# The order of softplus and a softmax split on ACT, and the queue of the state's first 128 rows

## The chip, the core and the metric

The kernel runs on one core of a Trainium2 chip. The metric is the time of one execution in microseconds, as the device measures it; the median of three runs stands for a kernel. The core's engines are TensorE (PE; its weight loads are shown as PEld), VectorE (DVE), ScalarE (ACT), GpSimd (POOL) and SyncE (SP). Each works through its own instructions in order and waits for the others by semaphores. DMA transfers are issued here from the queues of SP, ACT and POOL.

## What is computed

The reference has three stages on 8 images of 512 tokens with 512 features (8 heads of 64), and 32 state rows for each image:

```python
scores = scale * x @ state.T;  a = softmax(scores);   xread = a @ state     # per head
scores2 = scale * state @ x.T; a2 = softmax(scores2); sread = a2 @ x
x = concat([xread, sread])                     # 8 * (512 + 32) = 4352 rows of 512
h = x @ w_in;  g = max(h, 0) + log1p(exp(-abs(h)));  y = g @ w_out          # softplus MLP
logits = y @ w_gate     # each row goes to one of 8 experts, at most 544 rows each, greedily by logit
out = relu(y[rows] @ w1[e]) @ w2[e]            # per expert
```

Results are float32. The kernel gets that accuracy out of TensorE by splitting operands in two parts, `hi` and `lo`, and making three products: hi·hi, hi·lo and lo·hi.

## The kernel before, in words

**The middle stage.** The MLP runs in slots. Slot s is batch b = s // 16 (one image) and ft = s % 16 (128 of the 2048 hidden features). For a slot, `mlp1` makes the hidden values of 128 features and 512 tokens in a PSUM bank `p_h` with six matmuls (line 485). They aren't made from w_in but from the token softmax (`at_hi`, `at_lo`) and a product of state and w_in (`P_hi`, `P_lo`). There are two banks p_h, so that slots s and s + 2 share one. Softplus follows in three ACT operations and one on DVE: `softplus_abs` writes abs(h) to `t_sp` (line 520) and puts it on the list `waits`; `softplus_log` empties the list and makes Exp and Ln of each entry (lines 527 and 528); `softplus_b` makes g = max(h, 0) + t_sp on DVE (line 540), which is the last reader of the bank. ACT then copies g to `g_hi` (line 548), POOL makes `g_lo` = g − g_hi (line 551), and `mlp2` adds twelve matmuls into four banks p_y (lines 569, 571, 573).

**The order of the work** is that of the program: the loop over s (line 793) is written out by hand, and each engine executes what it is given in that order. For batches after the first, the body of slot s is, in short:

```python
softplus_b(s + 1); mlp1(s + 2); softplus_abs(s + 2)
if ft % 4 == 0: p_pair()                    # P_hi on ACT, P_lo on DVE (lines 454 to 462)
if ft in (ATT if b > 1 else ATT1): att_step(b)
softplus_log()                              # Exp and Ln of slot s + 2
mlp2(s)
```

`att_step` advances the attention of the next image by one step. For images 2 to 7 that is the generator `attention`, run during batches 1 to 6. Its steps are: scores; two steps that subtract the maximum and make Exp (these call `softplus_log` ahead of their own Exp); two steps that divide by the sum on DVE (lines 287 to 290), transpose into `back` on DVE (line 291), copy to `at_hi` on ACT (line 292) and make `at_lo` on POOL (line 293): these two are the splits of the token softmax, for the even and the odd heads; a step for the state softmax (maximum on DVE at lines 295 and 296, `softplus_log`, Exp on ACT at line 299, sums on DVE); transposes of it on TensorE (line 308); and the read of x by the state. In batches 2 to 6 the splits fall in slots ft = 7 and 8; in batch 1 they fall later, in slots 9 and 10. `at_hi` and `at_lo` of an image are read by `mlp1` of the next batch.

**The state rows.** The 256 rows of all states go through the MLP as a batch of their own, 128 rows (j = 0, 1) at a time. In the generator `mlp2_rest` (line 757) their pieces, each one block of 128 features for one j, run through `split_g` (ACT's g_hi, POOL's g_lo) and three matmuls (lines 576, 578, 580); the split of a piece is issued one piece ahead, and g_hi and g_lo have two buffers. Behind the last piece of each j, `y_state(j)` copies the bank to `yt` on DVE (line 631) and sends it to `y_d` in DRAM in four transfers of 64 KB, one for each image (line 634). These pieces are mixed by hand with the routing of the first expert (lines 912 to 1088), whose steps alternate between DVE and small matmuls. When the first expert is known, SP reads its number and loads its w1 (line 1106); when its rows are known, POOL gathers them from `y_d` (line 1122), which needs all rows of y to have landed. The expert stage follows.

Of the kernel before, what the change touches and what calls it, by code (L numbers as in the profile page):

```python
# [17 lines left out]
B, H, S, NS, D = 8, 8, 512, 32, 64  # L18
# [12 lines left out]
def attn_moe_kernel(ctx, tc, x_s, x_t, state_t, w_in, w_out, w_gate, w1, w2, out):  # L31
    nc = tc.nc
    V, A, G, PE, SP = nc.vector, nc.scalar, nc.gpsimd, nc.tensor, nc.sync
# [12 lines left out]
    def bg(kind=None):  # L46

        if turn_of[1]:
            turn_of[0] ^= 1
            kind = turn_of[0]  # L50
        return bank("bg1" if kind else "bg0")
# [76 lines left out]
    y_d = dram.tile([N, DM], F32, name="y_d")  # L128
# [86 lines left out]
    def ordered(x):  # L215

        return x.rearrange("p (j q c) -> p q j c", j=4, q=4)
# [34 lines left out]
    def attention(b):  # L252

        xT = XT.pop(b)
        ST = at.tile([128, 2, 512], F32, name="ST", tag="ST")
        Z = at.tile([128, 2, 512], F32, name="Z", tag="P1")
        m2 = at.tile([128, 2], F32, name="m2", bufs=2)
        s2 = at.tile([128, 2], F32, name="s2", bufs=2)
        hi = pt.tile([128, 2, 512], F32R, name="at_hi", bufs=2)
        lo = pt.tile([128, 2, 512], F32R, name="at_lo", bufs=2)  # L260
        AT[b] = (hi, lo)
        ps = bg(0), bg(1)
        for par in range(2):
            o = par * 64
            for hp in range(4):
                PE.matmul(ps[par][hp * 32:(hp + 1) * 32, :], stT[o:o + 64, b, hp, :], xT[o:o + 64, hp, :],
                          start=True, stop=True, tile_position=(o, hp * 32))
        for par in range(2):
            A.activation(ST[:, par], ps[par], AF.Copy)
        xt = at.tile([128, 4, DM], F32, name="xt", tag="x")  # L270
        SP.dma_start(xt, x_s[b].rearrange("(r p) c -> p r c", p=128))
        yield
        G3 = [128, 16, NS]
        for par in range(2):
            a3 = Z[:, par].rearrange("p (g n) -> p g n", n=NS)
            m1 = at.tile([128, 16], F32, name="m1", bufs=2)
            V.transpose(Z[:, par], ST[:, par])
            V.tensor_reduce(m1, a3, axis=AX, op=OP.max)
            V.tensor_tensor(a3, a3, m1[:, :, None].to_broadcast(G3), op=OP.subtract)
            softplus_log()  # L280
            A.activation(Z[:, par], Z[:, par], AF.Exp, scale=0.125)
            yield
        back = wk.tile([128, 2, 512], F32, name="back", tag="yst", bufs=4)
        for par in range(2):
            a3 = Z[:, par].rearrange("p (g n) -> p g n", n=NS)
            s1 = at.tile([128, 16], F32, name="s1", bufs=2)
            V.tensor_reduce(s1, a3, axis=AX, op=OP.add)
            V.tensor_scalar(s1, s1, 1e-9, None, op0=OP.add)
            V.reciprocal(s1, s1)
            V.tensor_tensor(a3, a3, s1[:, :, None].to_broadcast(G3), op=OP.mult)  # L290
            V.transpose(back[:, par], Z[:, par])
            A.activation(hi[:, par], back[:, par], AF.Copy)
            G.tensor_tensor(lo[:, par], back[:, par], hi[:, par].bitcast(F32), op=OP.subtract)
            yield
        V.tensor_reduce(m2, ST, axis=AX, op=OP.max)
        V.tensor_scalar(m2, m2, -0.125, None, op0=OP.mult)
        softplus_log()
        for par in range(2):
            A.activation(ST[:, par], ST[:, par], AF.Exp, bias=m2[:, par:par + 1], scale=0.125,
                         accum_out=s2[:, par:par + 1])  # L300
        V.tensor_scalar(s2, s2, 1e-9, None, op0=OP.add)
        V.reciprocal(s2, s2)
        yield
        A2 = at.tile([128, 2, 512], F32, name="A2", tag="P1")
        ps = bg(0), bg(1)
        for par in range(2):
            for r in range(4):
                PE.transpose(ps[par][:, r * 128:(r + 1) * 128], ST[:, par, r * 128:(r + 1) * 128], ident)
        for par in range(2):
            A.activation(A2[:, par], ps[par], AF.Copy)  # L310
        yield
        yield from state_read(b, A2, xt, s2)

    def state_read(b, A2, xt, s2):
        p = bg()
        for par in range(2):
            for r in range(4):
                for hp in range(4):
                    c0 = r * 128 + hp * 32
                    PE.matmul(p[hp * 32:(hp + 1) * 32, par * 64:(par + 1) * 64], A2[:, par, c0:c0 + 32],  # L320
                              xt[:, r, (2 * hp + par) * D:(2 * hp + par + 1) * D], start=(r == 0), stop=(r == 3))
        if b + 1 < B:
            load_xT(b + 1)
        sr = at.tile([128, 128], F32, name="sr")
        for par in range(2):
            V.tensor_scalar(sr[:, par * 64:(par + 1) * 64], p[:, par * 64:(par + 1) * 64], s2[:, par:par + 1],
                            None, op0=OP.mult)
        yield
        p = bg()
        PE.transpose(p[:, 0:128], sr, ident)  # L330
        V.tensor_copy(XsT[:, :, b * NS:(b + 1) * NS], p[:, 0:128].rearrange("p (h n) -> p h n", h=4))
# [192 lines left out]
    def softplus_log():  # L524
        while waits:
            t = waits.pop(0)
            A.activation(t, t, AF.Exp, scale=-1.0)  # L527
            A.activation(t, t, AF.Ln, bias=1.0)  # L528
# [100 lines left out]
    def y_state(j):  # L629
        t = wk.tile([128, 2, 512], F32, name="yt", tag="yst", bufs=4)  # L630
        V.tensor_copy(t[:, 0].rearrange("p (q j c) -> p q j c", q=4, j=4), ordered(yb[j]))
        for i in range(4):
            r0 = (4 * j + i) * TB + S
            (SP if i % 2 else A).dma_start(y_d[r0:r0 + NS], t[i * NS:(i + 1) * NS, 0])

    def logits(s, kind=None):
        b, ft = divmod(s, NFT)
# [119 lines left out]
    def mlp2_rest():  # L757
        todo = [(s, (0, 1, 2, 3)) for s in range(NX - LATE, NX)]
        todo += [(NX + ft, (j,)) for j in range(2) for ft in range(NFT)]

        def split(i):
            if i < len(todo):
                s, js = todo[i]
                split_g(s, late[s] if s < NX else stash["g"][:, s - NX], slice(js[0] * 128, js[-1] * 128 + 128),
                        LATE_ON[i] if i < LATE else "AG")

        split(0)
        yield
        for i, (s, js) in enumerate(todo):
            split(i + 1)  # L770
            while s == NX and len(lazy) > 3 - js[0]:
                lazy.pop(0)()
            if s == NX - 1:
                adds = y_out(B - 1, 0) + y_out(B - 1, 2)
            for j in js:
                for i_, _ in enumerate(mlp2_steps(s, (j,))):
                    if i_ == 2 and s == NX - 1:
                        lazy.append(adds[j])
                    yield
            if s == NSLOT - 1:  # L780
                y_state(js[0])
# [590 lines left out]
```

## Time and profile before

| | |
|---|---|
| median of 3 runs | 1225.92 us (1225.27 to 1227.36) |
| profiled execution | 1226.8 us, span 1225.0 us |
| busy share of the span | PE 95%, PEld 74%, DVE 54%, ACT 52%, POOL 40% |
| mean granted TensorE clock | 0.99 |
| instructions | 21305 |

The span runs from the first to the last instruction of the core; the execution's time has some 1.8 us more around it. An engine's busy time is the union of its instructions; matmuls are pipelined and their ends are modelled, so two that follow one another overlap in the rows. A timeline row is: start, duration, engine, line, operation, out<-in, shape, count, and in brackets the idle time of the engine before it with what ended it. A "q" behind an engine's name means its queue, which issues a transfer. A row of the costliest groups is: line, engine, operation, names, shape, count | busy us, mean ns of one | idle us before it, with what ended most of it. A granted clock of 1.00 is 2.4 GHz, one of 0.5 is 1.2 GHz.

### The profile page before, as it was taken

The numbers are of one execution on the slowest core, as the hardware profiler recorded it, in microseconds if no ns is written. First come the engines' busy times: TensorE is split into PE (matmuls) and PEld (weight loads), VectorE is DVE, ScalarE is ACT, GpSimd is POOL, SyncE is SP. The second block draws the span as 40 slices with busy tenths as digits, with TensorE's granted clock in tenths as the row PEclk, the third lists the DMA queues.
The fourth block names the chain that finished last, engine by engine and source line by source line (L and its number), as shares of the span: only waits on it lengthen the run. The fifth ranks groups of instructions, "written<-read, shape, count | busy, mean of one in ns | idle before, by whom it ended". The sixth has DMA issues, their size and how long they took to land.

```text
span 1225.0 us, 21305 instructions
## 1 busy us (share of the span) xinstructions
PE 1159.3 (95%) x8291; PEld 910.3 (74%) x8291; DVE 667.3 (54%) x1797; ACT 639.2 (52%) x1277; POOL 487.8 (40%) x466
## 2 busy tenths in 40 slices
PE   4898999999999999999999997999999999999996
PEld 1565676777677776777677765879797988789895
DVE  6998545353363543634434266777685868751120
ACT  3776656666666666666666732533343333333330
POOL 0334323222232232222344425645647555546531
PEclk9998999999999999999999998999999999999999
DMA  7463021111201112002000003251523415234200
GB/s 241 139 202 127 1 70 35 53 52 36 69 1 52 52 35 58 13 36 69 1 18 18 1 18 123 88 194 40 180 92 129 150 68 172 104 108 140 89 18 37
DMA packets 51061, 95.78 MB, mean 78 GB/s; under 512 B 4624, under 2 KB 19088, under 8 KB 50960
## 3 DMA queue, kind: packets, MB, share of 16 engines
q1 hardware_dynamic: 45136, 76.33, 18.8%
q0 software_dynamic: 5632, 17.83, 4.2%
q8 instruction: 65, 1.06, 0.4%
q10 hardware_dynamic: 192, 0.26, 0.1%
q14 instruction: 36, 0.29, 0.1%
HBM read 76.58 MB, written 17.83 MB: 77 GB/s over the span
## 4 chain that ended last, share of the span: by engine, by line
PE 66%; DVE 17%; ACT 7%; issue 6%; POOL 2%; DMA 1%; SPq 0%; ACTq 0%; POOLq 0%; DVEq 0%
PE p_y L1310 12%; PE p_h L485 10%; PE p_y L1265 6%; PE p_y L569 6%; PE p_y L571 5%; PE p_h L1265 5%; PE p_y L573 5%; PE p_bg L912 2%; DVE g L540 2%; PE p_y L576 2%; PE p_bg L454 2%; PE p_bg L496 2%; PE p_y L578 2%; PE p_y L580 2%; PE p_h L1176 1%
## 5 line engine op out<-in xcount | busy, mean ns | idle before, releaser
L551 POOL TENSOR_TENSOR g_lo<-g,g_hi 128x512 fp32r<-128x512 f32 x127 | 164.9, 1299 | 340.7 <-ACT g_hi L548 327.3
L569 PE MATMUL p_y<-g_hi,wo_hi 128*128 128x512 f32 x448 | 185.0, 413 | 0.0
L571 PE MATMUL p_y<-g_hi,wo_lo 128*128 128x512 f32 x448 | 177.7, 397 | 3.7 <-POOL wo_lo L232 3.7
L573 PE MATMUL p_y<-g_lo,wo_hi 128*128 128x512 f32 x448 | 177.2, 396 | 0.0
L540 DVE SCALAR_TENSOR_TENSOR g<-p_h,t_sp 128x512 f32<-128x512 f32 x128 | 87.7, 686 | 122.7 <-ACT t_sp L528 121.8
L548 ACT ACTIVATE g_hi<-g 128x512 fp32r<-128x512 f32 x126 | 79.6, 632 | 124.0 <-DVE g L540 95.2
L569 PEld LDWEIGHTS p_y<-g_hi,wo_hi 128*128 128x128 f32 x448 | 85.1, 190 | 48.3 <-issue 15.9
L485 PE MATMUL p_h<-at_hi,P_hi 128*128 128x512 f32 x256 | 104.9, 410 | 8.1 <-DVE g L540 8.1
L1310 PE MATMUL p_y<-w2h,h2h 128*128 128x512 f32 x256 | 105.1, 411 | 0.0
L485 PE MATMUL p_h<-at_hi,P_lo 128*128 128x512 f32 x256 | 101.8, 398 | 0.0
L485 PE MATMUL p_h<-at_lo,P_hi 128*128 128x512 f32 x256 | 101.7, 397 | 0.0
L1310 PE MATMUL p_y<-w2l,h2h 128*128 128x512 f32 x256 | 101.5, 396 | 0.0
L1310 PE MATMUL p_y<-w2h,h2l 128*128 128x512 f32 x256 | 101.3, 396 | 0.0
L571 PEld LDWEIGHTS p_y<-g_hi,wo_lo 128*128 128x128 f32 x448 | 85.4, 191 | 21.0 <-POOL wo_lo L232 4.9
L573 PEld LDWEIGHTS p_y<-g_lo,wo_hi 128*128 128x128 f32 x448 | 85.2, 190 | 21.0 <-POOL g_lo L551 2.4
L1318 POOL DMA_INDIRECT out_dram<-ot,idx x40 | 39.4, 985 | 145.6 <-ACT ot L1316 68.9
L1149 POOL TENSOR_TENSOR w2l<-s2w,w2h 128x512 fp32r<-128x512 f32 x64 | 82.5, 1305 | 14.2 <-ACT w2h L1148 13.0
L520 ACT ACTIVATE t_sp<-p_h 128x512 f32<-128x512 f32 x128 | 75.3, 588 | 24.5 <-PE p_h L485 24.2
L1149 POOL TENSOR_TENSOR w1l<-s1w,w1h 128x512 fp32r<-128x512 f32 x63 | 80.4, 1300 | 11.2 <-ACT w1h L1148 10.3
L528 ACT ACTIVATE t_sp<-t_sp 128x512 f32<-128x512 f32 x128 | 80.9, 632 | 4.1
L527 ACT ACTIVATE t_sp<-t_sp 128x512 f32<-128x512 f32 x128 | 80.6, 630 | 2.0
L1265 PE MATMUL p_y<-yTh,w1h 128*128 128x288 f32 (+1 forms) x256 | 76.9, 300 | 0.6 <-DVE h2t L1274 0.6
(284 smaller groups left out, 2643.5 us busy)
## 6 DMA issues: line engine op xcount, KB each, us to landing
s1w<-in_moe_w_dram SPq DMA_DIRECT2D x8, 2048.0 KB, 8.4
s2w<-in_moe_w_dram SPq DMA_DIRECT2D x8, 2048.0 KB, 9.5
st<-in_moe_w_in_dram SPq DMA_DIRECT2D x16, 512.0 KB, 4.1
xT<-in_x_t_dram SPq DMA_DIRECT2D x16, 512.0 KB, 4.4
st<-in_moe_w_out_dram SPq DMA_DIRECT2D x16, 512.0 KB, 3.7
xt<-in_x_s_dram SPq DMA_DIRECT2D x8, 1024.0 KB, 5.8
y_d<-yz SPq DMA_DIRECT2D x48, 128.0 KB, 3.6
y_d<-s_g SPq DMA_DIRECT2D x8, 128.0 KB, 2.2
```

Source lines behind the costliest of these rows:

```text
L485: PE.matmul(h, l[:, f0:f0 + 128], r[:, par, :], start=(n == 0), stop=(n == 5))
L527: A.activation(t, t, AF.Exp, scale=-1.0)
L528: A.activation(t, t, AF.Ln, bias=1.0)
L540: V.scalar_tensor_tensor(g[:, :w], hps.pop(s)[:, :w], 0.0, tsp.pop(s)[:, :w], op0=OP.max, op1=OP.add)
L548: A.activation(hi[:, c], g[:, c], AF.Copy)
L551: (G if on[1] == "G" else V).tensor_tensor(lo[:, c], g[:, c], hi[:, c].bitcast(F32), op=OP.subtract)
L569: PE.matmul(yb[j], wo_hi[:, ft, c], hi, start=st, stop=False)
L571: PE.matmul(yb[j], wo_lo[:, ft, c], hi, start=False, stop=False)
L573: PE.matmul(yb[j], wo_hi[:, ft, c], lo, start=False, stop=sp)
L1149: eng.tensor_tensor(lo, src, hi.bitcast(F32), op=OP.subtract)
L1265: PE.matmul(p[:, :w], l[:, k, f], r[:, k, c], start=(n == 0), stop=(n == 11))
L1310: PE.matmul(p, l[:, ft, c], r[:, ft, :], start=(n == 0), stop=(n == 23))
```

## The change

In the two split steps of `attention`, `softplus_log()` is called ahead of ACT's copy to `at_hi`, so that the pending Exp and Ln of slot s + 2 stand ahead of that copy in ACT's order; the call behind `att_step` then finds an empty list. In `y_state`, all four transfers for j = 0 are issued by SP (before: images 1 and 3 of the four by SP, 0 and 2 by ACT); for j = 1, SP issues 0 and 2 and ACT issues 1 and 3 (before: the other way round).

```diff
             V.transpose(back[:, par], Z[:, par])
+            softplus_log()
             A.activation(hi[:, par], back[:, par], AF.Copy)
             G.tensor_tensor(lo[:, par], back[:, par], hi[:, par].bitcast(F32), op=OP.subtract)
             yield
...
         V.tensor_copy(t[:, 0].rearrange("p (q j c) -> p q j c", q=4, j=4), ordered(yb[j]))
         for i in range(4):
             r0 = (4 * j + i) * TB + S
-            (SP if i % 2 else A).dma_start(y_d[r0:r0 + NS], t[i * NS:(i + 1) * NS, 0])
+            (A if j and i % 2 else SP).dma_start(y_d[r0:r0 + NS], t[i * NS:(i + 1) * NS, 0])
```

## Rows read from the trace of the kernel before

**Rows 1.** The page's first part: busy us, share of the span, instructions.
```profile
PE 1159.3 (95%) x8291; PEld 910.3 (74%) x8291; DVE 667.3 (54%) x1797; ACT 639.2 (52%) x1277; POOL 487.8 (40%) x466
```
**Rows 2.** Busy time by stretch: one batch, and the start of the expert stage.
```profile
core 0: us, PE busy (x) PEld busy (x) DVE busy (x) ACT busy (x) POOL busy (x), PEclk, DMA share, GB/s
...
503.00:581.00 78.00, 76.87 (x453) 56.40 (x452) 34.74 (x63) 50.66 (x95) 23.05 (x18) 1.00 0.12 41
...
757.00:775.00 18.00, 9.84 (x75) 8.54 (x72) 13.36 (x39) 5.68 (x11) 11.96 (x11) 0.72 0.63 191
```
**Rows 3.** The costliest groups: the first matmul of p_h.
```profile
L485 PE MATMUL p_h<-at_hi,P_hi 128*128 128x512 f32 x256 | 104.9, 410 | 8.1 <-DVE g L540 8.1
```
**Rows 4.** Line 292, what ended ACT's idle time before it (us, times).
```profile
  DVE back L291: 26.8, 12
```
**Rows 5.** Timeline of batch 6, second split: ACT, VectorE, POOL, then TensorE.
```profile
585.81 0.58 ACT L520 ACTIVATE t_sp<-p_h 128x512 f32<-128x512 f32 x1
...
590.92 0.63 ACT L292 ACTIVATE at_hi<-back 128x512 fp32r<-128x512 f32 x1 [3.05 <-DVE back L291]
...
592.84 0.69 DVE L540 SCALAR_TENSOR_TENSOR g<-p_h,t_sp 128x512 f32<-128x512 f32 x1 [1.95 <-ACT t_sp L528]
...
597.82 0.67 DVE L540 SCALAR_TENSOR_TENSOR g<-p_h,t_sp 128x512 f32<-128x512 f32 x1
...
591.63 1.28 POOL L293 TENSOR_TENSOR at_lo<-back,at_hi 128x512 fp32r<-128x512 f32 x1 [4.36 <-ACT at_hi L292]
...
592.35 0.39 PE L573 MATMUL p_y<-g_lo,wo_hi 128*128 128x512 f32 x1
593.59 0.50 PE L485 MATMUL p_h<-at_hi,P_hi 128*128 128x512 f32 x1 [0.85 <-DVE g L540]
...
595.09 0.39 PE L569 MATMUL p_y<-g_hi,wo_hi 128*128 128x512 f32 x1
595.32 0.39 PE L571 MATMUL p_y<-g_hi,wo_lo 128*128 128x512 f32 x1
595.72 0.50 PE L573 MATMUL p_y<-g_lo,wo_hi 128*128 128x512 f32 x1
...
597.91 0.40 PE L573 MATMUL p_y<-g_lo,wo_hi 128*128 128x512 f32 x1
598.55 0.50 PE L485 MATMUL p_h<-at_hi,P_hi 128*128 128x512 f32 x1 [0.25 <-DVE g L540]
```
**Rows 6.** Timeline of batch 6, first split: ACT's copy and VectorE's next g.
```profile
582.54 0.63 ACT L292 ACTIVATE at_hi<-back 128x512 fp32r<-128x512 f32 x1 [1.43 <-DVE back L291]
...
584.46 0.69 DVE L540 SCALAR_TENSOR_TENSOR g<-p_h,t_sp 128x512 f32<-128x512 f32 x1 [1.96 <-ACT t_sp L528]
```
**Rows 7.** Timeline of batch 1: TensorE's two pauses behind its splits.
```profile
210.31 0.50 PE L485 MATMUL p_h<-at_hi,P_hi 128*128 128x512 f32 x1 [1.11 <-DVE g L540]
...
218.20 1.06 PE L308 MATMUL p_bg<-ident,ST 128*128 128x128 f32 x8 [0.87 <-DVE P_lo L462]
```
**Rows 8.** Timeline around `y_state(0)`: VectorE, ACT with its queue, SP's queue, TensorE.
```profile
743.13 0.69 DVE L631 COPY yt<-p_y 128x512 f32<-128x512 f32 x1
743.85 0.84 ACTq L634 DMA_DIRECT2D y_d<-yt  x2
744.79 0.51 ACT L548 ACTIVATE g_hi<-s_g 128x128 fp32r<-128x128 f32 x2 [3.06 <-DVE yt L631]
...
750.14 0.41 SPq L1106 DMA_DIRECT2D s1w<-in_moe_w_dram  x1
...
743.40 0.40 PE L580 MATMUL p_y<-wo_hi,g_lo 128*128 128x512 f32 x1
745.16 0.49 PE L576 MATMUL p_y<-wo_hi,g_hi 128*128 128x512 f32 x1 [1.36 <-ACT g_hi L548]
```
**Rows 9.** Timeline at `y_state(1)`: the two queues' issues.
```profile
757.24 1.19 SPq L634 DMA_DIRECT2D y_d<-yt  x2
757.25 1.39 ACTq L634 DMA_DIRECT2D y_d<-yt  x2
```

## The prediction

> **What bounds the kernel now.** The page comes first: TensorE is busy 95% of the span [rows 1]. An average hides stages, so the table of stretches comes next [rows 2]. In one batch of the middle stage (503 to 581 us) TensorE is busy 76.87 of 78 us at a granted clock of 1.00, ACT 50.66, VectorE 34.74, POOL 23.05. No other engine is near its limit, so there is nothing to win but TensorE's own pauses and nothing to lose unless another engine makes it wait. Which pauses? The costliest groups name one: the first matmul of p_h (line 485) was idle for 8.1 us, all of it until VectorE had written g [rows 3]. I then looked for who makes g late. The split of the token softmax (line 292) holds ACT idle for 26.8 us in 12 places, waiting for the transpose `back` [rows 4]. Twelve is two splits in each of six batches (b = 1 to 6, which prepare images 2 to 7).
>
> The timeline of one such batch joins the two [rows 5]. ACT finishes Abs of slot 10 by about 586.4, then copies P, and is idle from 587.87 (590.92 less 3.05). The split's copy stands next in its queue and can't start until 590.92. Exp and Ln of slot 10 stand behind it, though their input was ready more than 4 us before. VectorE has finished `back` just ahead of 590.92 and idles 1.95 us until Ln ends; it writes g at 592.84 to 593.53. TensorE needs that, because p_h has two banks and the matmuls of slot 12 take the bank that g of slot 10 reads. It starts at 593.59.
>
> **What TensorE loses there.** Matmuls of this kind start 0.23 us apart (595.09 to 595.32), so a pause is the distance of two starts less 0.23; the first matmul after a pause also lasts 0.50 instead of 0.40, which I count as 0.10 more. All in [rows 5]:
> - 592.35 to 593.59: 1.24 − 0.23 = 1.01, and 0.10: 1.11 (waits for g of slot 10).
> - 595.32 to 595.72: 0.17, and 0.10: 0.27 (waits for g_lo of slot 10, made late by the same g).
> - 597.91 to 598.55: 0.41, and 0.10: 0.51 (waits for g of slot 11, which ends at 598.49).
> Sum 1.89 us. I take the other batches but the first as alike: 0.85 and 0.25 us of idle, five times, make 5.5 of the 8.1 in [rows 3]. Batch 1 does its attention steps later and adds 1.11 [rows 7]; what is left, some 1.4, lies ahead of these batches.
>
> **The change, part one: Exp and Ln ahead of the split.** It adds and removes no operation. In 12 places two ACT operations of 0.63 us move ahead of one copy, and the flush at the end of the slot then finds nothing to do.
>
> First split of a batch [rows 6]: the copy starts at 582.54 after 1.43 us of idle, and Exp and Ln need 1.28, so they fit into the idle and the copy loses nothing. g of slot 9, at 584.46 after 1.96 us of waiting, comes at about 582.5. TensorE doesn't wait for that one today, so I count 0; it is slack for the next slot.
>
> Second split: Exp and Ln fit into 3.05 us of idle, g of slot 10 follows `back` at about 590.9 and ends at 591.6. TensorE wants the bank at 592.35 + 0.23 = 592.58: a full us to spare. The 1.11 goes.
>
> What is late next? On ACT g_hi of slot 10 follows the split's copy and ends near 592.3. POOL makes at_lo from 591.63 for 1.28 us, and g_lo of slot 10 queues behind it: at the 1.28 of its neighbour, 592.95 to 594.25. TensorE wants it at 595.55 − 1.11 = 594.44. This is the tightest place, 0.2 us; of the 1.96 us by which the first split's g comes earlier some should reach it, but I don't count on that. I take the 0.27 as gone. g of slot 11 moves with g of slot 10 by 1.95, to 596.54; TensorE wants it at 598.14 − 1.38 = 596.76. I take the 0.51 as gone too. The bounds for these two are 0 and 0.78 per batch. Nothing else is queued behind the split's copy that anybody needs soon: at_hi and at_lo are read one batch later.
>
> Five batches: 5 × 1.89 = 9.45. Batch 1 [rows 7]: 1.11 of idle before the matmul at 210.31, with the 0.16 by which the modelled end of a matmul (0.39) runs beyond its 0.23 and 0.10 for the first matmul, is 1.37; the transposes at 218.20 wait for P_lo 0.87 + 0.16 = 1.03, P_lo being late because the same chain made ACT's P copies late. Here g moves by nearly 2 us at both splits, so I count both: 2.40. Part one: 11.85 us, with 1.11 × 5 + 1.37 = 6.92 as the lower bound if only the first pause goes.
>
> **Part two: the state's rows.** For the first 128 rows two of four transfers move from ACT's queue to SP's; for the second 128 each queue keeps two, exchanged. The row that matters is ACT's next split of g: it starts at 744.79 after 3.06 us of idle that ended with the copy to yt at 743.13 to 743.82, and two issues of 0.84 us together [rows 8]. TensorE's next piece waits for it: 743.40 to 745.16 is 1.76, less 0.23 is 1.53, and 0.10 for the first matmul: 1.63. Without the issues ACT waits neither for yt nor for them, and its split follows the matmul that frees g_hi, as in the pieces before. The routing chain, whose matmul of `sat` stands behind it on TensorE, comes earlier by the same. Taken: 1.63.
>
> The price is on SP: four issues at some 0.4 us end near 745.5. Behind them stands the load of the first expert's w1 at 750.14 [rows 8], some 748.5 when all has moved. So they hide in 3 us of an idle queue; without that cover they would cost 0.8. The second 128 rows: SP's pair takes 1.19 us and ACT's 1.39 [rows 9], so the exchange moves the last landing, for which the gather waits, by 0.2 either way; I take 0.
>
> The Trainium skill's page "DMA: Bandwidth & Descriptors", section "Issuing engines are not separate DMA queues", says that a second issuing engine saves only the sequencer's time of issuing. By that rule the move is worth ACT's 0.84 us at most and costs SP as much; the rows differ, because ACT's issues also wait for yt with g_hi behind them.
>
> **Sum:** 11.85 + 1.63 = 13.48, taken as 13.5. The profiled execution took 1226.8 us, 0.9 above the median of the runs, 1225.92. So 1213.3 for a profiled execution and **1212.4** for the median.
>
> **The rivals.**
> - *Only the first pause goes.* POOL's queue or the chain of g of slot 11 stays as late as now: 6.92 + 1.63 = 8.55, 1217.4 us. For it: only 0.2 us to spare at two points. Against: what the first split gives comes on top.
> - *Part two saves issue time alone.* ACT's split would be late for another reason: 11.85 + 0.84 = 12.7, 1213.2. Against: the split of every other piece comes in time without it.
> - *Part one does nothing.* If the list of pending operations were empty at the split, only part two is left: 1224.3. Against: Abs stands ahead of the copy and g waits for Ln behind it [rows 5].
> - *Slower, by the clock.* The granted clock falls to 0.72 on average at 757 to 775 [rows 2], which is half speed (1.2 of 2.4 GHz) for 10 of 18 us; TensorE is busy for 9.84 of them. Everything is moved by 13.5 us, so the clock could come back later than the matmuls. Matmuls at half speed lose half their time: from 27 us of dense matmuls at 1.2 GHz on, the gain is lost; with 40 us it is 1225.9 − 13.5 + 20 = 1232.4. Against: 8 us of this stretch are at full speed already, and nothing in the change lengthens the wait in it.
>
> **How the numbers follow.** Forecast 0.67, issue time alone 0.08, first pause alone 0.16, nothing from part one 0.05, slower 0.04. The forecast's own spread is some 2 us, mostly the stretch at half clock: 1210 to 1214.5. The range reaches to the first rival, 1210 to 1218. What a measurement can tell from no change is about 0.2%, 2.5 us: the first three cases are faster by more, 0.91; the fourth is the same by it, 0.05; the last slower, 0.04.
>
> **What would show it.** Right: in the changed profile ACT's copy of line 292 follows Ln; its idle time falls from 26.8 to some 11 us; the 8.1 us of [rows 3] fall to about 1.4; a batch is 1.9 us shorter; in the batch's waits neither g_lo nor P_lo takes TensorE's time; the matmul of the second state half follows without 1.36 us of idle; SP issues four transfers in a row. Wrong: a new TensorE wait for g_lo at the third matmul of a slot, a P copy or g still late after the split, w1 of the first expert landing later against the routing, or a stretch at half clock behind 775 us.

## The result and the profile after

| | before | changed |
|---|---|---|
| median of 5 runs each, side by side | 1227.09 us (1225.27 to 1227.69) | 1214.73 us (1214.45 to 1214.99) |
| profiled execution, span | 1225.0 us | 1212.9 us |
| mean granted TensorE clock | 0.99 | 0.988 |

The ratio is 0.9902 with a 95% interval of 0.9888 to 0.9915: faster by 12.4 us in the medians and by 12.1 in the two spans. The forecast was 13.5 faster, 1212.4 us.

The page of the changed kernel, its first part and the group that answers to [rows 3] (all its line numbers from 292 on are one higher):

```profile
PE 1156.4 (95%) x8291; PEld 913.0 (75%) x8291; DVE 663.3 (55%) x1797; ACT 641.0 (53%) x1277; POOL 488.6 (40%) x466
...
L486 PE MATMUL p_h<-at_hi,P_hi 128*128 128x512 f32 x256 | 103.9, 406 | 1.4 <-DVE g L541 1.4
```

The idle time ahead of the first matmul of p_h has gone from 8.1 to 1.4 us. The table of stretches for [rows 2], with the columns as there: first a stretch of one batch's length, taken 7 us earlier, then the start of the expert stage:

```profile
496.00:574.00 78.00, 78.00 (x462) 58.21 (x461) 35.23 (x64) 52.52 (x98) 23.80 (x19) 1.00 0.13 41
...
744.00:763.00 19.00, 10.81 (x66) 9.64 (x67) 13.21 (x38) 5.70 (x11) 12.98 (x11) 0.64 0.61 183
```

In 78 us TensorE is now busy for all 78.00 (76.87 before) and makes 462 matmuls instead of 453. The second row is no better than before: the mean granted clock is 0.64 over 19 us where it was 0.72 over 18.

What ended ACT's idle time before the split's copy, for [rows 4]:

```profile
  DVE back L291: 11.7, 7
```

The timeline of batch 6 in the changed kernel, second split, for [rows 5] (ACT and VectorE, then POOL, then TensorE):

```profile
577.97 0.63 ACT L529 ACTIVATE t_sp<-t_sp 128x512 f32<-128x512 f32 x1
579.73 0.71 DVE L291 STREAM_TRANSPOSE back<-Z 128x512 f32<-128x512 f32 x1
580.36 0.65 DVE L541 SCALAR_TENSOR_TENSOR g<-p_h,t_sp 128x512 f32<-128x512 f32 x1
580.47 0.63 ACT L293 ACTIVATE at_hi<-back 128x512 fp32r<-128x512 f32 x1 [1.87 <-DVE back L291]
...
581.18 1.30 POOL L294 TENSOR_TENSOR at_lo<-back,at_hi 128x512 fp32r<-128x512 f32 x1 [5.25 <-ACT at_hi L293]
582.44 1.30 POOL L552 TENSOR_TENSOR g_lo<-g,g_hi 128x512 fp32r<-128x512 f32 x1
...
582.49 0.39 PE L574 MATMUL p_y<-g_lo,wo_hi 128*128 128x512 f32 x1
582.72 0.40 PE L486 MATMUL p_h<-at_hi,P_hi 128*128 128x512 f32 x1
584.35 0.40 PE L572 MATMUL p_y<-g_hi,wo_lo 128*128 128x512 f32 x1
584.58 0.39 PE L574 MATMUL p_y<-g_lo,wo_hi 128*128 128x512 f32 x1
```

Ln ends at 578.60, VectorE writes g straight behind `back`, and the copy comes last. The two pauses of TensorE are gone: 582.49 to 582.72 and 584.35 to 584.58 are both the plain 0.23.

The state's last piece of the first 128 rows, for [rows 8] (VectorE, ACT, SP's queue, TensorE):

```profile
731.20 0.31 ACT L549 ACTIVATE g_hi<-s_g 128x128 fp32r<-128x128 f32 x1 [1.23 <-PE p_y L579]
731.37 0.69 DVE L632 COPY yt<-p_y 128x512 f32<-128x512 f32 x1
732.09 1.75 SPq L635 DMA_DIRECT2D y_d<-yt  x4
736.70 0.41 SPq L1107 DMA_DIRECT2D s1w<-in_moe_w_dram  x1
...
731.64 0.39 PE L581 MATMUL p_y<-wo_hi,g_lo 128*128 128x512 f32 x1
731.86 0.39 PE L577 MATMUL p_y<-wo_hi,g_hi 128*128 128x512 f32 x1
```

ACT splits g before the copy to yt has even begun, the matmul follows after 0.22, and SP's four issues end at 733.84, 2.86 us ahead of the next thing in its queue.

**The two traces laid side by side.** The matmuls are the same 8291 in the same order, so each can be compared with its own counterpart. The table sums up by how much a matmul starts earlier (−) or later (+) in the changed trace:

| where (start before → after) | step | stands at |
|---|---|---|
| up to batch 1 | +0.16 | +0.16 |
| batch 1: 210.31 → 209.29, 218.20 → 216.05 | −1.18, −1.13 | −2.15 |
| batches 2 to 6, five times −1.10, −0.25, −0.56 | −9.54 | −11.69 (598.55 → 586.86) |
| second half of the state: 745.16 → 731.86 | −1.60 | −13.29 |
| first gathered rows: 764.68 → 752.49 | +1.11 | −12.19 |
| matmuls at half clock, up to 771.38 → 760.18 | +0.99 | −11.20 |
| matmul of `sat`: 773.90 → 761.80 | −0.90 | −12.10, and so to the end |

Each row gives the shift at the matmul named. Since the first matmul behind a pause lasts longer, the shift settles some 0.1 us further in the next few matmuls: it is −2.20 behind batch 1, −11.74 ahead of the state's second half and −13.39 ahead of the first gathered rows.

The gain was all there and 1.2 us of it was lost again at the start of the expert stage. The timeline there, changed kernel: the last copy to yt with ACT's issues behind it, two VectorE operations of the routing (`oh`, and `mk`, which compares scores `v` with thresholds `thr`), POOL's `w1l` (the lo part of the expert's first weights) and the first gather:

```profile
743.12 0.69 DVE L632 COPY yt<-p_y 128x512 f32<-128x512 f32 x1
743.85 1.41 ACTq L635 DMA_DIRECT2D y_d<-yt  x2
...
746.03 0.44 DVE L985 TENSOR_TENSOR oh<-oh,code 128x272 f32<-128x272 f32 x1
746.07 1.52 POOL L1150 TENSOR_TENSOR w1l<-s1w,w1h 128x512 fp32r<-128x512 f32 x1 [3.53 <-ACT w1h L1149]
...
747.81 1.24 DVE L1016 TENSOR_TENSOR mk<-v,thr 128x1054 bf16<-128x1054 f32 x1
747.88 2.18 POOL L1123 DMA_INDIRECT xg<-y_d,idx  x1 [0.29 <-DVE ohu L990]
```

and the kernel before:

```profile
756.52 0.69 DVE L631 COPY yt<-p_y 128x512 f32<-128x512 f32 x1
...
761.15 1.14 POOL L1122 DMA_INDIRECT xg<-y_d,idx  x1 [0.18 <-issue]
761.20 1.24 DVE L1015 TENSOR_TENSOR mk<-v,thr 128x1054 bf16<-128x1054 f32 x1
```

Before, POOL's first gather starts 0.05 us ahead of VectorE's mk and takes 1.14; after, it starts 0.07 behind it and takes 2.18. The 0.12 us of order cost 1.04, and the five gathers run one after another, so the later ones, and the transposes of their rows on TensorE, are late by about the same.

### The profile page after: what moved, and what is told of

It reads as the page before. It is cut to its first block, busy times and chain, and to the rows that moved or that the text cites. A ratio compares the mean times of both kernels' runs of the same rounds, so it can differ in the third digit from the quotient of the medians.

```text
span 1212.9 us, 21304 instructions
## 1 busy us (share of the span) xinstructions
PE 1156.4 (95%) x8291; PEld 913.0 (75%) x8291; DVE 663.3 (55%) x1797; ACT 641.0 (53%) x1277; POOL 488.6 (40%) x466
## 4 chain that ended last, share of the span: by engine, by line
PE 77%; DVE 12%; issue 6%; POOL 2%; ACT 1%; DMA 1%; SPq 0%; POOLq 0%; DVEq 0%; ACTq 0%
PE p_h L486 13%; PE p_y L1311 12%; PE p_y L570 8%; PE p_y L572 8%; PE p_y L574 8%; PE p_y L1266 6%; PE p_h L1266 5%; PE p_bg L455 2%; PE p_bg L913 2%; PE p_y L577 2%; PE p_bg L497 2%; PE p_y L579 2%; PE p_y L581 2%; PE p_h L1177 1%; DVE c_a L193 1%
## 5 line engine op out<-in xcount | busy, mean ns | idle before, releaser
L1150 POOL TENSOR_TENSOR w1l<-s1w,w1h 128x512 fp32r<-128x512 f32 x63 | 80.4, 1300 | 11.3 <-ACT w1h L1149 10.4
```

The lines of the kernel that those rows point to most:

```text
L1150: eng.tensor_tensor(lo, src, hi.bitcast(F32), op=OP.subtract)
```

## The experiments

Two questions were open: whether each part gives what the forecast gave it, and what made the first gather late. A useful measure for the second, free of everything ahead of it, is the time from the last copy to yt until the end of the span: 1225.0 − 756.52 = 468.5 us before, 1212.9 − 743.12 = 469.8 after. In the traces of the last two sessions this stretch also holds pauses near 960 us, whether a gather was held or not ("What stays open"). Free of these too is the distance from that copy to the matmul of `sat` (a step of the routing), where the table ends: 773.90 − 756.52 = 17.38 before, 761.80 − 743.12 = 18.68 after. The runs were made in three sessions, each on one chip with its own runs of the kernel before; a ratio compares within a session.

### One part at a time

First the order of the softplus alone, the line of `y_state` as before:

```diff
-            (A if j and i % 2 else SP).dma_start(y_d[r0:r0 + NS], t[i * NS:(i + 1) * NS, 0])
+            (SP if i % 2 else A).dma_start(y_d[r0:r0 + NS], t[i * NS:(i + 1) * NS, 0])
```

> Part one alone (the queues of the state rows as before). The forecast's theory: TensorE's pauses in batches 1 to 6 are gone, the pause of 1.36 us at the second state half is back; 11.7 us less than before, by what the traces of before and after show up to 600 us: ratio 0.9905. If the two parts help each other (part one's gain needs part two), less than 11 us. Theory of the late gather (the first gather on POOL starts just behind VectorE's mk and is held by it, because the second state half's rows land later): with the old queues the first gather takes 1.1 to 1.2 us, not 2.2.

Measured: 1215.18 us against 1227.3, ratio 0.9901 (0.9886 to 0.9916): 12.1 us faster. TensorE's timeline at the second half of the state:

```profile
732.40 0.39 PE L581 MATMUL p_y<-wo_hi,g_lo 128*128 128x512 f32 x1
734.15 0.50 PE L577 MATMUL p_y<-wo_hi,g_hi 128*128 128x512 f32 x1 [1.37 <-ACT g_hi L549]
```

The pause of [rows 8] is back, to 0.01 us (1.75 from start to start). The first gather took 1.14 us here, and from the copy to yt to the end it is 1214.1 − 745.49 = 468.6, as before (17.43 to `sat`).

Then the queues alone, in the kernel before:

```diff
-            (SP if i % 2 else A).dma_start(y_d[r0:r0 + NS], t[i * NS:(i + 1) * NS, 0])
+            (A if j and i % 2 else SP).dma_start(y_d[r0:r0 + NS], t[i * NS:(i + 1) * NS, 0])
```

> Part two alone. If its two effects are the 1.6 us pause that goes and a first gather of 2.2 us in place of 1.1: 0.5 us less than before, which can hardly be told from no change. If the long gather has nothing to do with the queues: 1.6 us less, and a first gather of 1.1 us. If the move saves issue time alone: 0.8 us less, with TensorE's pause halved and not gone.

Measured: 1225.83 us, ratio 0.9991 (0.9982 to 1.0): 1.5 faster in the medians, which the interval just allows to be nothing; matmul by matmul its trace gains 1.63 at the second half of the state. The two parts sum to 12.1 + 1.5 = 13.6 us, the forecast's 13.48.

### Is it the exchange of the second 128 rows?

Theory: the exchanged queues land the rows otherwise and move the steps at the expert's start. Rival: the exchange does nothing and only a shift of some 0.1 us between POOL and VectorE decides. The changed kernel with the second 128 rows sent as before:

```diff
-            (A if j and i % 2 else SP).dma_start(y_d[r0:r0 + NS], t[i * NS:(i + 1) * NS, 0])
+            (A if j and i % 2 == 0 else SP).dma_start(y_d[r0:r0 + NS], t[i * NS:(i + 1) * NS, 0])
```

> The changed kernel with the queues of the second 128 state rows exchanged back (ACT sends 0 and 2, SP 1 and 3); the first 128 stay with SP. Theory that the exchange made the last row land 0.14 us later against the routing and so let mk start ahead of the gather: first gather 1.1 us, about 1.1 us below the changed kernel, 1213.6. Rival, that the long gather is an accident of the shift by 13 us or of the longer half clock: first gather 2.2 us, time as the changed kernel, 1214.7.

Measured: 1213.61 us, ratio 0.9895 (0.9879 to 0.991). The timeline (VectorE, POOL):

```profile
746.79 1.14 POOL L1123 DMA_INDIRECT xg<-y_d,idx  x1 [0.44 <-DVE oh L985]
...
747.74 1.25 DVE L1016 TENSOR_TENSOR mk<-v,thr 128x1054 bf16<-128x1054 f32 x1
748.23 1.58 POOL L1123 DMA_INDIRECT xg<-y_d,idx  x1 [0.31 <-issue]
```

The first gather is short again, but now the second meets mk and takes 1.58 instead of 0.95; from the copy to yt to the end it is 1211.3 − 742.20 = 469.1. By itself that would fit the theory; the run of the queues alone speaks against it, since it has the exchange and a first gather of 1.14 and a second of 1.51 (1223.7 − 754.72 = 469.0). So the changed kernel itself was run once more in a later session, to see whether its trace repeats:

> The changed kernel once more, beside the one with thresholds in PSUM on the same chip. Theory that a hold between VectorE and POOL decides by some 0.1 us, as it falls in a run: from the last copy to yt to the end of the span 468.5 to 469.8 us, the long end when the first gather starts behind mk. Rival, that the exchange of the queues fixes it: the first gather is 2.2 us again and the end 469.8, 1214.7.

Measured: 1216.78 us against 1230.32, ratio 0.9894 (0.9876 to 0.9911). Its timeline:

```profile
745.47 1.30 POOL L1150 TENSOR_TENSOR w1l<-s1w,w1h 128x512 fp32r<-128x512 f32 x1 [3.27 <-ACT w1h L1149]
745.68 1.38 DVE L985 TENSOR_TENSOR oh<-oh,code 128x272 f32<-128x272 f32 x1
...
747.28 1.14 POOL L1123 DMA_INDIRECT xg<-y_d,idx  x1 [0.51 <-DVE oh L985]
...
748.16 1.25 DVE L1016 TENSOR_TENSOR mk<-v,thr 128x1054 bf16<-128x1054 f32 x1
748.73 1.51 POOL L1123 DMA_INDIRECT xg<-y_d,idx  x1 [0.31 <-issue]
```

The same program, and this time the first gather is short and the second is held; to `sat` it is 760.50 − 742.79 = 17.71, where the changed kernel's first trace needed 18.68. The theory falls: which of the two starts first is not fixed by the exchange, and not even by the program; it differs from execution to execution.

What it goes with can be read in the eleven traces.

- **When mk starts.** In five traces (before, changed, order alone, first split alone, and the second run of the thresholds in PSUM below) it starts 4.68 to 4.72 us behind the last copy to yt, in the other six 5.37 to 5.53. In the six, POOL's w1l starts 0.01 to 0.21 ahead of VectorE's oh (L985 above), and oh takes 1.38 to 1.54 us; in the five it starts 0.02 to 0.34 behind, and oh takes 0.44. POOL's w1l waits for ACT's w1h, which stands behind ACT's two issues, and these took 1.39 to 1.71 us in the five and 1.15 to 1.35 in the six.
- **When the first gather starts.** In all eleven it starts 0.84 to 0.96 us behind the last landing of the rows of y. That landing comes 3.54 to 4.04 us behind the copy: 3.67 before, 3.81 in the first trace of the changed kernel and 3.54 in its second.

So the forecast was right that the gather waits for the landing. But the landing and the issues move by some tenths of a us between executions of one program, and with them the order of two pairs, POOL's w1l with VectorE's oh and POOL's gather with VectorE's mk. Among the five traces with an early mk, the first gather starts 0.05 us ahead of mk in the two with the old queues and 0.07 to 0.22 behind it in the three with the exchange; five traces can't tell whether the exchange has a part in that.

### Is it VectorE's mk that holds the gather?

If the two exclude each other because mk reads both operands from SBUF, then mk with its thresholds in PSUM should leave the gather alone, wherever it starts. The first step's thresholds are copied once into a PSUM tile:

```diff
     V.tensor_copy(iof_t, iof)
+    thr0_t = small(31, sci)
+    V.tensor_copy(thr0_t.bitcast(F32), thr0.bitcast(F32))
...
-                thr = thr0
+                thr = thr0_t if ph else thr0
```

> The changed kernel with the first digit's thresholds of phases 1 to 7 read from a PSUM copy, so that mk has one operand in SBUF instead of two; its start and length stay as they were. Theory that mk with two SBUF operands holds POOL's gather: the first gather takes about 1.1 us although it starts behind mk, and the time is 1.1 us below the changed kernel, 1213.6. Rival, that the gather is long for another reason (a queue, the clock, any busy VectorE): still 2.2 us, 1214.7.

Measured: 1213.11 us, ratio 0.9891 (0.9876 to 0.9906). From the copy to yt to the end it is 1210.7 − 742.20 = 468.5, the 468.5 of the kernel before. The timeline:

```profile
746.67 1.14 POOL L1125 DMA_INDIRECT xg<-y_d,idx  x1 [0.44 <-DVE oh L987]
...
747.62 1.24 DVE L1018 TENSOR_TENSOR mk<-v,p_bg 128x1054 bf16<-128x1054 f32 x1
748.12 0.95 POOL L1125 DMA_INDIRECT xg<-y_d,idx  x1 [0.31 <-issue]
```

The second gather starts 0.50 behind mk, as in the kernel with the second rows as before (0.49), and takes 0.95 where that took 1.58. In the later experts the changed kernel has gathers of 1.21, 1.20, 1.76 and 2.01 us, each started while such a mk was running; all four are gone. But here the first gather happened to start ahead of mk, so the case of 2.18 was not met. The same kernel was run again beside the changed one:

> Thresholds in PSUM once more, on the same chip as the changed kernel. Theory of the hold by two SBUF operands: no gather that starts behind mk is longer than 1.1 us in any phase, the end of the span 468.5 us behind the last copy to yt, and 0.5 to 1.3 us below the changed kernel. Rival, that the lower time of the first run came from the chip: no difference between the two.

Measured: 1216.01 us, ratio 0.9884 (0.9866 to 0.9901). The timeline:

```profile
747.29 1.24 DVE L1018 TENSOR_TENSOR mk<-v,p_bg 128x1054 bf16<-128x1054 f32 x1
747.43 1.14 POOL L1125 DMA_INDIRECT xg<-y_d,idx  x1 [0.36 <-DVE ohu L992]
```

Now the first gather starts 0.14 behind mk, between the 0.07 and the 0.22 at which it took 2.18 (changed kernel) and 2.04 (first split alone, below), and takes 1.14. The hold is mk's second operand in SBUF; that is shown. To `sat` this trace needs 760.06 − 742.61 = 17.45 us, as the traces without a hold do (17.38 and 17.43), against 17.71 of the changed kernel beside it, which had only its second gather held, by 0.56. That the version is faster as a whole is not shown: it is 0.8 us below the changed kernel in this pair of medians, with intervals that overlap, and from the copy to yt to the end both traces take 471.2 to 471.3, with the pauses near 960 us in that stretch.

### Which of the two splits gives the gain?

Only the first split's Exp and Ln moved ahead, then only the second's:

```diff
-            softplus_log()
+            if par == 0:
+                softplus_log()
```

> The changed kernel, but Exp and Ln go ahead of the copy in the first split of each image alone. By the forecast's steps the first split's earlier g gives TensorE nothing itself and comes through only as slack; in the changed kernel the second split's copy stands 0.6 us earlier against the first than before. So each of batches 2 to 6 should gain about 0.6 us (the first pause shrinks from 1.0 to 0.4, the others stay), 3 to 4 us in all: about 1223. Rival, that the first split gives nothing at all: part two alone, 1225.8. Rival, that it gives most: below 1219.

Measured: 1225.27 us against 1228.6, ratio 0.997 (0.9958 to 0.9981): 3.3 faster. TensorE's timeline in batch 6, and POOL's first gather with mk:

```profile
588.62 0.39 PE L575 MATMUL p_y<-g_lo,wo_hi 128*128 128x512 f32 x1
589.26 0.50 PE L487 MATMUL p_h<-at_hi,P_hi 128*128 128x512 f32 x1 [0.26 <-DVE g L542]
...
755.17 1.24 DVE L1017 TENSOR_TENSOR mk<-v,thr 128x1054 bf16<-128x1054 f32 x1
755.39 2.04 POOL L1124 DMA_INDIRECT xg<-y_d,idx  x1 [0.45 <-DVE ohu L991]
```

The first pause shrinks from 1.01 to 0.41 (588.62 to 589.26, less 0.23), and the other two stay. A batch gains 0.56 instead of 1.91: the first split's earlier g passes down the chain to the second split's, but no further. The first gather is held here too: 2.04 us, starting 0.22 behind mk, and to `sat` it is 769.05 − 750.49 = 18.56. Up to the last copy to yt this trace gains 756.52 − 750.49 = 6.03 us, and the medians show 3.3; of the difference the held gather accounts for 1.2, and the rest was not followed up. Then the second split alone:

```diff
-            softplus_log()
+            if par == 1:
+                softplus_log()
```

> The changed kernel, but Exp and Ln go ahead of the copy in the second split alone. By the forecast's steps the second split alone frees the bank a full us before TensorE wants it, and g_lo of slot 10 and g of slot 11 come 0.2 us before they are wanted: all three pauses gone, a batch as short as in the changed kernel, 1214.7. Rival, that the two tight places need what the first split gives: the first pause goes, up to 0.78 us per batch stays, up to 1218.6.

Measured: 1215.84 us, ratio 0.9895 (0.9879 to 0.9912): 12.8 faster. POOL's and TensorE's timeline in batch 6:

```profile
582.42 1.29 POOL L553 TENSOR_TENSOR g_lo<-g,g_hi 128x512 fp32r<-128x512 f32 x1
...
583.98 0.39 PE L575 MATMUL p_y<-g_lo,wo_hi 128*128 128x512 f32 x1
586.26 0.40 PE L487 MATMUL p_h<-at_hi,P_hi 128*128 128x512 f32 x1
```

The matmuls of batches 2 to 6 gain 1.09 to 1.11, 0.25 and 0.56 again. g_lo ends at 583.71, 0.27 us ahead of the matmul that reads it at 583.98: the forecast's 0.2 us of spare time without the first split's help. So the second split carries all of it in these batches, and the first one is slack. In batch 1 it is not quite so: either split alone ends the first pause (the shift settles 1.36 and 1.37 further), but at the second pause the first split alone gains 0.17, the second alone 0.51, and both together 1.08.

### How much does ACT's queue cost TensorE?

If ACT's split of g stands behind the wait for the copy to yt and behind the issues as well, four issues on ACT must cost TensorE that wait and twice the issues:

```diff
-            (A if j and i % 2 else SP).dma_start(y_d[r0:r0 + NS], t[i * NS:(i + 1) * NS, 0])
+            (A if j == 0 or i % 2 else SP).dma_start(y_d[r0:r0 + NS], t[i * NS:(i + 1) * NS, 0])
```

> The changed kernel with all four transfers of the first 128 state rows on ACT's queue (before: two, changed: none). Theory that ACT's split of g stands behind both the wait for yt and the issues: TensorE's distance of starts there is 1.76 with two issues and 0.23 with none; with four it is 1.76 + 0.8 = 2.56, and the time is 2.3 us above the changed kernel, 1217.0. If only the wait for yt counts and the issues run beside: 1.76, 1216.3. If issue time alone counts, twice the 0.84: 1216.4 with a distance of 1.9.

Measured: 1219.29 us, ratio 0.9928 (0.9911 to 0.9945), 3.4 above the run with the second split alone, of the same session and with the same queues for the second rows. ACT and its queue, then TensorE:

```profile
731.73 1.78 ACTq L635 DMA_DIRECT2D y_d<-yt  x4
733.61 0.51 ACT L549 ACTIVATE g_hi<-s_g 128x128 fp32r<-128x128 f32 x2 [4.00 <-DMA y_d<-yt]
...
731.27 0.40 PE L581 MATMUL p_y<-wo_hi,g_lo 128*128 128x512 f32 x1
733.97 0.50 PE L577 MATMUL p_y<-wo_hi,g_hi 128*128 128x512 f32 x1 [2.30 <-ACT g_hi L549]
```

The pause is 733.97 − 731.27 = 2.70 from start to start, 2.57 by the forecast's way of counting (less 0.23, and 0.10). That is 0.94 more than with two on ACT, which is what two more issues last (1.78 − 0.84). But the time is 3.4 us up where 2.3 were expected, because the pause has a sequel in the table of stretches:

```profile
731.20:735.08 3.88, 1.58 (x7) 0.83 (x7) 0.76 (x4) 0.79 (x3) 0.87 (x2) 1.00 0.26 68
735.08:738.50 3.42, 3.42 (x9) 2.32 (x8) 1.74 (x12) 0.65 (x3) 1.37 (x3) 0.50 0.00 0
```

For 3.42 us the granted clock is 0.50, 1.2 GHz, and matmuls start 0.43 apart instead of 0.23. Matmul by matmul against the run with the second split alone, the pause with its slow first matmuls adds 2.58 and the half clock behind it 1.56, 4.14 in all; the spans differ by 4.1 (1217.8 − 1213.7) and the medians by 3.4.

## Why the prediction was right, point by point

**The middle stage: right, to 0.2 us.** The three terms of a batch, 1.11, 0.27 and 0.51, measured 1.10, 0.25 and 0.56; 9.45 for the five batches measured 9.54. Batch 1's 2.40 measured 2.31 by the table, and 2.45 where the shift has settled. Reading a pause as the distance of two starts less the 0.23 of its neighbours, with 0.10 for the first slow matmul, thus gave each to 0.05 us, while the idle time of the rows alone (0.85 and 0.25 in [rows 5]) gives 1.1 of 1.9. The idle of the split's copy was to fall to some 11 us and is 11.7; the 8.1 of [rows 3] was to fall to 1.4 and did.

**The tightest place: right, with more to spare than was said.** g_lo was forecast at 594.25 against 594.44, 0.2 to spare. In the changed trace it ends at 583.74 and is wanted at 584.58: 0.84. The run with the second split alone, where nothing is on top, has 0.27. So the margin of 0.2 was well counted for the second split, and the rest is what the first one passes on, which the forecast did not count on. The first rival (only the first pause goes, 8.55 us) falls: neither g_lo nor g of slot 11 is late, even with the second split alone.

**The first split: 0 counted, and it is 0 in these batches** as long as the second one moves. Alone it gives 0.56 a batch. In batch 1, where both were counted, both are needed.

**The state's rows: right.** 1.63 forecast, 1.60 measured, and the pause of 1.37 came back when the line did. The rival by issue time alone, 0.84, falls, since ACT's program is in order and its split of g stood behind an issue that waited for the copy to yt. The Trainium skill's page "DMA: Bandwidth & Descriptors", section "Issuing engines are not separate DMA queues", counts only the sequencer's time of issuing as saved by a second issuing engine; this trace differs, with 1.60 for issues of 0.84. That the cost is wait and issue together is shown by four on ACT: two more issues add 0.94. SP hid its four, with 2.86 us to spare where "3 us" was said.

**The second 128 rows: the term that was mis-sized.** The step reads: "so the exchange moves the last landing, for which the gather waits, by 0.2 either way; I take 0". In the profiled execution the start of the expert stage measured +1.19 us by the table (−13.29 to −12.10). The terms that were priced came to 2.31 + 9.54 + 1.60 = 13.45 against 13.48; 13.45 less 1.19, and less the 0.16 that the execution was late ahead of batch 1, is the 12.1 of the spans. The landing moved within what the forecast said: 3.67 us behind the copy to yt before and 3.81 after, and the gather began 0.13 us later by the copy (4.63 and 4.76). The step that failed is from there to the time: the forecast passed the landing's shift on as it was, and left out that POOL's gather then falls behind the start of VectorE's mk and is held by it. The rows for it stood in the trace of before: the gather at 761.15, mk at 761.20, 0.05 apart. And in the later experts of the kernel before there are gathers of 1.76 and 2.01 us, held by such a mk. A shift of 0.1 us could therefore cost from 0 to about 1.2, the length of mk, and not 0.2. That is the bound that this term should have had. That this execution paid 1.3 us to `sat` (18.68 against 17.38) and a later one of the same program 0.3 (17.71) is luck, and the forecast came so close partly because the loss is small beside the gain.

**The clock: no lasting cost.** What the rival "slower, by the clock" feared did appear: the half clock lasted 13.65 us (746.67 to 760.33) instead of 10.24 (759.19 to 769.43). TensorE's longer wait for the first rows (idle 2.32 against 1.12) does not explain it: the trace of the order alone, with a short first gather, has 13.66 us, and that of the first split alone, with a held one, 10.24. The longer half clock took 0.99 us from the matmuls that ran under it, and the next wait, for `sat` at 773.90 in the trace before, gave 0.90 back: TensorE had stood idle for 1.04 there, and comes without a pause now. With the order alone, 13.66 us at half clock leave `sat` 17.43 behind the copy, against 17.38 with 10.24: the wait for `sat` takes the loss up.

**The total.** In the medians it is 12.4 faster (by the ratio 10.4 to 13.7), in the spans 12.1; 13.5 was forecast. Where the profile shows a short first gather the medians are nearer to the forecast: 13.6 by the two parts run alone, 1227.3 − 1213.61 = 13.7 with the second rows sent as before, 1230.32 − 1216.78 = 13.5 for the changed kernel in its later session. The medians hold other executions beside the profiled one, so this is a hint and no proof that the gather makes the difference.

**What stays open.** Why ACT's two issues behind the last copy to yt take 1.15 to 1.71 us and why the last rows land 3.54 to 4.04 behind it, in traces of which two pairs are of one program each (the changed kernel 1.41 and 1.15, the thresholds in PSUM 1.23 and 1.57); how often each order falls was not counted. What makes the half clock of the expert stage 10.24 us in some traces and 13.65 in others is open as well. In the later two sessions the traces show extra pauses of TensorE near 960 us, put down to "issue" and to no releaser (0.36 and 1.05 us in the changed kernel's), and 470.9 to 472.0 us stand there from the copy to yt to the end for 468.5 to 469.8; this was not followed up, and traces of different sessions are not compared in their ends.

## What to carry to other kernels

An engine that works in order should get the work that is ready ahead of the instruction that waits for another engine; the gain is TensorE's pause, read as the distance between starts, and not the waiting engine's idle time: ACT's 26.8 us in front of the splits went with 11.85 us of pauses. For a DMA issue on a busy engine, count what the issue waits for and what is queued behind it, and not only its own duration (0.84 of the 1.60 us here). And when everything downstream moves by the same amount, look for pairs of operations of two engines that start within a few tenths of a us of each other and of which one can hold the other up, and bound the cost by the length of the one that holds.

## What the runs showed of the hardware that was not expected

**A gather on POOL was held by a VectorE operation with both its operands in SBUF.** An indirect gather that starts behind mk takes 2.18 us (0.07 behind), 2.04 (0.22 behind), 1.58 (0.49) and 1.51 (0.57), and 0.88 to 1.14 where no mk is running as it starts. The held one ends 0.8 to 1.0 us after mk wherever it began (749.05 and 750.06; 756.41 and 757.43; 749.41 and 750.24). With one operand of mk in PSUM it takes 1.14 (0.14 behind) and 0.95 (0.50 behind). In the other direction VectorE's oh takes 0.44 us, but 1.38 to 1.54 where POOL's w1l started 0.01 to 0.21 ahead of it. The Trainium skill's page "SBUF — State Buffer", section "Who interferes with whom", says that a VectorE instruction with two SBUF inputs contends with a GpSimd instruction that reads SBUF, and that the order of issue decides who blocks. The gather behind mk and oh behind w1l agree; a gather that started 0.05 us ahead of mk left mk at its 1.24 us. Of a tensor_tensor beside descriptor generation the page infers that it does not stall it, since that needs the write interface; mk is a tensor_tensor, and the gather, which takes its row numbers from `idx`, was held.

**The same program, two orders.** In the changed kernel the first gather started 0.07 us behind mk in one execution and 0.88 ahead of it in another (747.28 and 748.16). A single trace shows one of them, and an edit can look guilty of what a second trace of the same kernel does not show, as the exchange of the queues did here.

**A pause of 2.30 us of TensorE was followed by 3.42 us at 1.2 GHz, one of 1.36 was not.** Both stand in the same place of the program, between the last piece of the first 128 rows and the next, with matmuls 0.23 apart ahead of them: behind either pause the next starts of the state's matmuls are 0.27 to 0.34 apart three times; then they go back to 0.23 or 0.24 behind the shorter one, at a granted clock of 1.00, and to 0.43 behind the longer one, at 0.50 from 735.08, 1.11 us after the pause ended. So a wait can cost more than its length: 1.56 us behind 2.58 here, in the one trace of this kind.
